# Top-k attention with a squared-ReLU MLP on one core: threshold searches dropped, GpSimd's sums re-laid, and the third replacement of 81 groups moved to SIGN and a product

## The chip, the cores and the metric

One core of a Trainium2 chip runs the whole program. The metric is device time in microseconds; lower is better. The engines are named as in the profile: PE (TensorE matmuls; PEld its weight loads), DVE (VectorE), ACT (ScalarE), POOL (GpSimd), SP (SyncE, which issues DMAs).

## The reference

Inputs are q, k, v of shape (8, 8, 576, 64) and two weights, 512 x 2048 and 2048 x 512, all float32.

```python
scores = scale * np.matmul(q, k.transpose(0, 1, 3, 2))      # 64 heads of 576 x 576
kth = np.partition(scores, -32, axis=-1)[..., -32:-31]      # each row's 32nd largest
scores = np.where(scores >= kth, scores, -1e9)
attn = softmax(scores)
x = (attn @ v), heads side by side                          # 4608 x 512
out = (np.maximum(x @ w_in, 0.0) ** 2) @ w_out              # 4608 x 512
```

## The kernel before, in words

**Groups.** The 36,864 rows of scores go in 144 groups of 256: 128 partitions hold one row of each of two heads (or, for the 64 rows left over of every head, two pairs of heads). A group's scores are 128 x 2 x 576 float32. `top_k` finds each row's 32nd largest value, the threshold `kth`; `attend` transposes the scores on PE, adds a mask (made by ACT with RELU against the threshold, L1051) and takes EXP on ACT; `fetch`, `gather` and `collect` multiply by v and normalise; `feed` runs the MLP on 256 or 128 tokens at a time, ACT taking RELU (L1242), and the square made by POOL (L1257) or ACT (L1260) as a string of letters, `SQUARES`, says.

**The order of the work.** The program is planned before it is built. Every operation is given an engine, an assumed duration, a due time and its dependencies; `Plan.schedule` walks through time, gives each engine the ready operation that is due first, and so fixes the order on every engine and every buffer. Semaphore waits are put in from the dependencies. Group n is due at `T0 + PER * n`; each kind of operation has an offset, and a further one for each of 16 stages of the run (the table `AHEAD`). PE gets filler matmuls where it would stand idle, until a time near the end.

**A threshold.** A group's tile `s` holds in each row the 576 scores and, behind them, scratch areas. The 576 scores of a row are seen as four quarters of 144.
- PE writes the scores to PSUM and ACT copies them to `s` (L820).
- DVE folds the quarters with three maximum operations (L975): `m0`, `m1`, `big`. The last is the list of 144 column maxima.
- POOL finds what the folds lost, the three lists of smaller values, without comparisons: as 32-bit integers, max + min equals the sum of the two. The first wide operation (u<-s) adds the sources of all three folds to a buffer `u`, the second (s<-u,s) subtracts the three maxima. Each is one operation over 128 x 2 x 3 x 144 elements (both L970).
- DVE takes the eight largest of the maxima (MAX8, L1014), replaces them by a very small number (L1018: a load of eight values and a MATCH_REPLACE8), and does the same two more times, over 92, 112 and 147 columns; ahead of the third time it takes the eight largest of two of the smaller lists (L1009) into the list. A last MAX8 (L1021) gives ranks 25 to 32, and so the threshold.

Tiles `s` lie in a ring of six; a group starts at column `z`, which grows smaller each time round, so that a few columns of every group are left for a check at the end.

**The searched groups.** Eight of the 144 groups (`HUNT`) get no lists. `hunt` starts from the root mean square of a row, and ACT counts, five times for each row, how many scores exceed a trial threshold: SIGN over 583 columns with its accumulator (L845); POOL corrects the trial between counts with small operations on two columns (L852). POOL then multiplies signs and scores (L884), and DVE takes eight values (L886) and picks the threshold among them. These tiles are `hs` and `hz`.

**The verdict.** At the end DVE checks all rows (ties, lists that were too short, sums that overflowed) into one flag. Where the flag is set, a plain second pass over everything follows.

Of the kernel before, what the change touches and what calls it, by code (L numbers as in the profile page):

```python
# [6 lines left out]
ALU = mybir.AluOpType  # L7
# [6 lines left out]
P = 128  # L14
# [9 lines left out]
SLAST = 760  # L24
# [4 lines left out]
SEEN = {"pe": 0.02, "act": 0.0, "dve": 0.0, "gp": 0.045, "sp": 0.08}  # L29
# [368 lines left out]
def bass_top_k_attn__then__act_relu_squared_kernel(  # L398
# [24 lines left out]
    def sb(name, shape, dt=FP32, n=None):  # L423
# [4 lines left out]
    PER = 5.247  # L428
# [8 lines left out]
    MASKS = "aaaaaaaaaaaaaaaaaaaaaaaaaaaaaaaaaaaaaaaaaaaaaaaaaaaaaaaaaaaaaaaaaaaaaaaaaaaaaaaaaaaaaaaaaaaaaaaaaaaaaaaaaaaaaaaaaaaaaaaaaaaaaaaaaaaaaaaa"  # L437
    SQUARES = "gggaggggagggagagaaggggaaggagggggaggagggagaggaaaggagggaggggggggagggaggg"
    OWN = 2
# [9 lines left out]
    WLAST = 753  # L449
# [3 lines left out]
        "av": (-25.3, -1.5, -9, -43, -22.8, -25.3, 0.1, -9.5, 17.8, -35.8, -26.9, 4.1, -14.2, -32.1, -43, -36.6),  # L453
        "copy": (-37.1, -30.2, 19, 22.4, -11.3, -34.5, 11.2, -32.3, 43.2, 43.4, 40.5, -36.4, -9, 33.4, 34.6, 45),
        "drain": (-26, 19.3, 2.6, -34.3, -16.5, 27.3, 3.4, 27.5, 3.3, 26.3, 20.3, 28.4, -43.8, -21.9, -12.4, -27.9),
        "dup": (11.7, -10, 39.6, -15.3, 40.5, 32.2, 19.9, -27.9, 37.3, -15.6, 20.8, 45, -28.9, -25.5, 29, -45),
        "end": (6.6, -7.4, 42.5, -6.2, 12.6, 35, -27.3, -13.8, -23.7, 33.7, -13.8, -11.4, -8.7, -4.4, 9.6, 18.8),
        "exp": (-12.6, -0.1, -1.1, 11.7, -11.3, -29.4, -34.4, -19.1, -11.6, -25, 7.3, 38, 19.6, 5, 22.9, 13),
        "flip": (31.6, 10.7, 14.8, -18.1, -5.6, 4.6, 41.2, -42, -40.4, -23.4, -45, 8.7, -0.5, -30.9, -43.6, -4.2),
        "fold": (-45, -32.8, -42.9, -45, -40.2, -37.7, -37.1, -24.2, -42.3, -45, -44, -31.1, -45, -42, -45, -45),  # L460
        "found": (-6.1, -10.4, -34, 23.1, 31.8, 41.7, -30.8, -23.3, -21.7, 27.5, -42.4, -34.7, -42.2, -28.9, -37.3, -42.4),
        "fourth": (-20.5, -19.8, -30.9, -10.8, -40, 20.2, -45, -10.8, -8.5, -14.6, 36.7, -28.1, -16.3, 10.7, -40.2, -7.6),
        "h": (-45, 12, -42.9, -14.4, 2.9, 23.4, 43.2, -44.5, 18, 29.8, -28.3, -14.7, 14.3, 3.5, 27.2, -23.5),
        "last": (-45, -31, -32.6, -7.3, -45, 10.3, -13.8, -45, -43, -44.6, -37.2, -39.6, 20.4, -28.9, -29.6, -44.6),
# [39 lines left out]
    HN, HA, HP, HZ, HS, HD, HO = 0.269, 0.86, 0.68, 2.18, 4.728, 29.47, 23.95  # L504
# [17 lines left out]
    c24 = sb("c24", [P, 2, NGRP + 8])  # L522
    rzall = sb("rzall", [P, NALL])
    HUNT = {(0, 2, 3): 12, (1, 2, 3): 12, (2, 2, 3): 12, (3, 2, 3): 12, (4, 2, 3): 12, (5, 2, 3): 12, (6, 2, 3): 12, (7, 0, 1): 12}
    NH = len(HUNT)
    NSTEP = 4
    GAIN, NRAW = (.016, .008, .0075, .0045), 2
    START, ROUND, ODD, FAR = 1.68, 1.5 * 2.0 ** 27, 7, 2.0 ** 53
    hk = sb("hk", [P, 12 * NSTEP + 4 + 6 + 64])
    hth = sb("hth", [P, 2, NH])  # L530
    htt = sb("htt", [P, 2, NH])
    fh = sb("fh", [P, 2, 2, NH])
    hot = sb("hot", [P, 20 + 2 * NSTEP])
    fone = sb("fone", [P, 8])
# [10 lines left out]
        "s": ([P, 2, WIDE], FP32, NF), "hs": ([P, 2 * S + 16], FP32, 2), "hz": ([P, 2 * S + 20], FP32, 1), "u": ([P, 2 * (HALF + QUART) + 4], FP32, 1), "a": ([P, 2, 8], FP32, 2),  # L545
# [5 lines left out]
    pools = {nm: Pool(nm, spec[2], turn=nm == "s") for nm, spec in sizes.items()}  # L551
# [17 lines left out]
    def at(t):  # L569
        x = mem[t.pool.name][t.slot]  # L570
        if t.pool.name in ("hs", "hz"):
            c = 8 if t.pool.name == "hs" else 10
            return x[:, c:c + 2 * S].rearrange("p (i c) -> p i c", i=2)
# [77 lines left out]
    def build(full, weights, pl):  # L651
        state = {"h": 0, "n": 0, "u": 0, "pairs": 0, "last": {}}
        kths, rzs, checks, sought = [], [], [], {}
# [129 lines left out]
        def score(gi, qks, tg, st, early=False):  # L783
# [17 lines left out]
            def scores_z():  # L801
                o = banks(ss)
                for i, j in ((0, 0), (0, 1), (1, 1), (1, 0), (2, 0), (2, 1), (3, 1), (3, 0)):
# [13 lines left out]
                  take=[ss, st], tiled=True)  # L817
# [5 lines left out]
            if early:  # L823
                return ss, [copied(0, QUART)], lambda after: copied(QUART, S, after=after)
            cp = [copied(0, S)]
            return ss, cp, None

        def hunt(k, gi, qks, tg, due):

            st, hz = tile("hs"), tile("hz")  # L830
            score(gi, qks, tg, st)
            used = [0]

            def small(n_):
                used[0] += n_
                return lambda a=0, b=n_, c=used[0] - n_: hk[:, c + a:c + b]

            def wider(t, i, n_, more):
                x = mem[t.pool.name][t.slot]
                c = 8 if t.pool.name == "hs" else 10  # L840
                return x[:, c + S * i - ODD * (more and i == 0):c + S * i + n_ + ODD * (more and i == 1)]

            def look(j, func, acc, after, bias=None, n_=S):
                kw = [dict() if bias is None else dict(bias=bias(i, i + 1), scale=-1.0) for i in range(2)]
                return [pl.op("act", HA - (S - n_) / 1200 - .09 * (j == 0), pl.at("look", due + HO + HS * j + .1 * i), lambda i=i: act.activation(  # L845
                    wider(hz, i, n_, j > 0), wider(st, i, n_, j > 0), func, accum_out=acc(i, i + 1), **kw[i]),
                    r=[st], after=after,
# [806 lines left out]
```

## Time and profile before

| | |
|---|---|
| three runs | 775.69, 775.81, 777.02 us (median 775.81) |
| the profiled run | 775.29 us, of which the span from first to last instruction is 773.4 us |
| busy: DVE, ACT, POOL, PE | 732.4, 732.5, 702.5, 706.3 us |
| granted TensorE clock | 1.00 throughout |

How the rows are read. In a table of stages a row has the stretch, its length and each engine's busy time with its count of instructions in brackets. In a table of groups a row has the line, the engine, the operation, output <- inputs, shapes and count; then the busy time in us and the mean duration in ns; then the engine's idle time just before these instructions, with what ended it. In a timeline a row has the start, the length, the engine and the operation, "x2" for two neighbours merged. A wait's row has who waited for whom, the us in total, how often, and the longest.

### The profile page before, as it was taken

Reading aid. Unit: us, or ns where it says so; the run is one execution under the profiler, and the core shown is the slowest. Engines: PE = TensorE matmul, PEld = TensorE weight load, DVE = VectorE, ACT = ScalarE, POOL = GpSimd, SP = SyncE. Lnnn points to the kernel's source line nnn. Section 1 sums busy time; section 2 is a strip of 40 time slices with the busy share of each in tenths; the row PEclk is TensorE's granted clock in tenths of the full one; section 3 lists DMA queues with packets and bytes.
Section 4 is the critical chain, followed back from the end, with each engine's and each line's share of the span. In section 5 each row is a group of like instructions: output and inputs, shape, how many; then the busy total and the mean of one; then the engine's idle time right before and its main releaser. Section 6 shows DMA issues by size and latency. Waiting matters only on the chain.

```text
span 773.4 us, 28086 instructions
## 1 busy us (share of the span) xinstructions
PE 706.3 (91%) x10764; PEld 531.8 (69%) x10764; DVE 732.4 (95%) x3504; ACT 732.5 (95%) x1173; POOL 702.5 (91%) x635
## 2 busy tenths in 40 slices
PE   7777789989998989898899999999999989999999
PEld 4555676657776676675777768677667766777676
DVE  5899999999999999999999999899999999999976
ACT  4899999999999999999999999999999999999994
POOL 3899999999989899899989999899998999999982
DMA  7677442253322451115512353123531144111111
GB/s 170 162 166 166 127 104 66 45 89 91 69 57 35 86 108 37 32 30 101 114 34 60 61 115 64 44 43 59 111 69 43 28 88 75 33 31 29 41 36 34
DMA packets 171578, 57.04 MB, mean 74 GB/s; under 512 B 156592, under 2 KB 163760, under 8 KB 171440
## 3 DMA queue, kind: packets, MB, share of 16 engines
q1 hardware_dynamic: 163376, 50.93, 28.2%
q0 software_dynamic: 7392, 4.13, 4.6%
q8 instruction: 84, 1.38, 0.8%
q14 instruction: 54, 0.44, 0.2%
q10 hardware_dynamic: 672, 0.16, 0.1%
HBM read 40.83 MB, written 13.57 MB: 70 GB/s over the span
## 4 chain that ended last, share of the span: by engine, by line
DVE 35%; POOL 30%; ACT 18%; issue 9%; PE 6%; DMA 1%; SPq 0%; POOLq 0%; DVEq 0%; ACTq 0%
POOL u L970 11%; POOL s L970 10%; DVE s L1018 10%; DVE s L975 8%; DVE c L1014 7%; PE ps L642 5%; DVE s L1009 5%; ACT s L820 4%; DVE kth L1021 4%; ACT w L1051 4%; POOL g L1257 3%; ACT p L1119 3%; ACT hz L845 2%; ACT g L1242 2%; POOL hk L852 2%
## 5 line engine op out<-in xcount | busy, mean ns | idle before, releaser
L970 POOL TENSOR_TENSOR u<-s 128x864 int32<-128x864 int32 x134 | 272.0, 2030 | 35.5 <-DVE s L975 32.0
L970 POOL TENSOR_TENSOR s<-u,s 128x864 int32<-128x864 int32 x134 | 229.5, 1713 | 5.3 <-DVE kth L1021 0.4
L1051 ACT ACTIVATE w<-s,kth 128x576 bf16<-128x576 f32 x270 | 212.1, 825 | 0.6 <-DVE kth L1021 0.4
L1018 DVE MATCH_REPLACE8 s<-c,s 128x92 f32<-128x92 f32 (+2 forms) x816 | 212.5, 268 | 0.0
L1014 DVE MAX8 c<-s 128x8 f32<-128x92 f32 (+2 forms) x816 | 194.1, 271 | 0.1
L642 PE MATMUL ps<-qk 64*128 64x384 f32 (+3 forms) x1280 | 178.3, 426 | 15.7 <-DVE s L975 14.0
L975 DVE TENSOR_TENSOR s<-ps,s 128x288 f32<-128x288 f32 x402 | 179.1, 446 | 7.7 <-ACT s L820 6.8
L1119 ACT ACTIVATE p<-ps 128x1152 bf16<-128x1152 f32 x144 | 168.8, 1173 | 1.7 <-PE ps L642 1.7
L820 ACT COPY s<-ps 128x1152 f32<-128x1152 f32 (+1 forms) x137 | 157.2, 1148 | 8.5 <-PE ps L642 7.6
L642 PEld LDWEIGHTS ps<-qk 64*128 64x128 f32 (+1 forms) x1280 | 129.6, 175 | 47.2 <-DVE s L975 23.0
L642 PE MATMUL ps<-wo,g 128*128 128x512 bf16 (+1 forms) x592 | 141.9, 375 | 2.4 <-ACT av L1187 1.0
L642 PE MATMUL ps<-xt,win 128*128 128x256 bf16 (+1 forms) x1280 | 131.8, 252 | 11.1 <-DMA xt<-x 3.9
L642 PEld LDWEIGHTS ps<-xt,win 128*128 128x128 bf16 x1280 | 97.5, 98 | 33.4 <-ACT g L1242 5.5
L1021 DVE MAX8 kth<-s 128x8 f32<-128x296 f32 x272 | 116.0, 458 | 0.0
L1009 DVE MAX8 s<-s 128x8 f32<-128x288 f32 x272 | 113.7, 451 | 0.0
L645 PEld LDWEIGHTS ps<-ident,s 64*128 64x128 f32 x2448 | 96.5, 139 | 24.6 <-ACT p L1119 8.6
L645 PE MATMUL ps<-ident,s 64*128 64x64 f32 x2448 | 103.4, 226 | 5.1 <-ACT p L1119 4.0
L1257 POOL TENSOR_TENSOR g<-g 128x1024 bf16<-128x1024 bf16 x50 | 94.8, 1896 | 4.9 <-ACT g L1242 4.9
L1242 ACT ACTIVATE g<-ps 128x512 bf16<-128x512 f32 x140 | 87.3, 654 | 3.7 <-PE ps L642 3.6
L642 PEld LDWEIGHTS ps<-wo,g 128*128 128x128 bf16 x592 | 50.9, 98 | 53.1 <-issue 4.1
L1018 DVE MATCH_VALUE_LOAD s<-c,s 128x8 f32 x816 | 65.6, 80 | 12.4 <-POOL s L970 12.1
L642 PE MATMUL ps<-vb,p 128*128 128x65 bf16 (+1 forms) x1600 | 63.0, 195 | 7.8 <-ACT g L1242 3.9
(111 smaller groups left out, 789.9 us busy)
## 6 DMA issues: line engine op xcount, KB each, us to landing
out_dram<-o SPq DMA_DIRECT2D x32, 256.0 KB, 2.3
rk<-in_k_dram SPq DMA_DIRECT2D x63, 128.0 KB, 2.6
rq<-in_q_dram SPq DMA_DIRECT2D x62, 128.0 KB, 2.6
s<-s SPq DMA_DIRECT2D x136, 32.0 KB, 1.9
g<-in_moe_w_in_dram SPq DMA_DIRECT2D x8, 512.0 KB, 4.6
g<-in_moe_w_out_dram SPq DMA_DIRECT2D x8, 512.0 KB, 4.6
vd<-in_v_dram POOLq DMA_DIRECT2D x14, 288.0 KB, 4.4
vb<-vd SPq DMA_DIRECT2D x56, 64.0 KB, 2.3
```

Of the source, the lines that this page charges most:

```text
L642: return pe.matmul(o, l, r, start=start, stop=stop, skip_group_check=True)
L645: return pe.matmul(o, i, ident, is_transpose=True, skip_group_check=True, **kw)
L820: return pl.op("act", .14 + 2 * (c1 - c0) / 1200, pl.at("copy", tg - LEAD + 1), lambda: act.copy(at(st)[:, :, c0:c1], two(banks(ss)[:, FIR ...
L970: return pl.op("gp", dur, prio, lambda: gp.tensor_tensor(o().bitcast(I32), x().bitcast(I32), y().bitcast(I32), op), **kw)
L975: return dve(.36, lambda: vec.tensor_tensor(o(), two(banks(ss)[:, FIRST_AT + c:], SECOND, QUART), x(), ALU.max), r=[ss], **kw)
L1009: prev[i] = [dve(.065 + HALF / 960, lambda i=i: vec.max(area(LIST, LIST + 8, i), area(LESS, LESS + HALF, i)), after=prev[i] + [low], hold= ...
L1014: lambda i=i, t=t, c0=c0, c1=c1: vec.max(eighth(t, i), area(c0, c1, i)),
L1018: lambda i=i, t=t, c0=c0, c1=c1: vec.match_replace(area(c0, c1, i), eighth(t, i), area(c0, c1, i), NEG), hold=[st])]
L1021: ks.append(chain(kth, i, prev[i], .065 + (8 + HALF) / 960, lambda i=i: vec.max(eighth(kth, i), area(BIGS - QUART, LIST + 8, i)), hold=[st]))
L1051: masks[i:] = [pl.op("act", .77, pl.at("mask", tw + .8 * i), lambda i=i: act.activation(at(wt)[:, i, :], at(st)[:, i, 0:S], ACTF.Relu, bia ...
L1119: return act.activation(at(pt)[:, :, :].rearrange("p c (h q) -> p h c q", h=2), bass.AP(x.tensor, x.offset, [x.ap[0], [APART, 2], [64, 9], ...
L1257: pl.op("gp", .12 + 1024 / 580, pl.at("square", tf + lag + 1), lambda g=g: gp.tensor_tensor(at(g)[:, :], at(g)[:, :], at(g)[:, :], ALU.mul ...
```

## The change

- The searches go, with their tiles, constants and small operations: all 144 groups find their threshold from lists.
- The ring of tiles `s` has seven places instead of six, in one tensor; `u` has two buffers instead of one. The scratch areas stand 194 columns apart instead of 192, and the two rows of a tile are 1250 columns apart instead of 1247.
- POOL's first wide operation now subtracts (each fold's larger source minus its result), and the second adds the other source. So the first needs all three folds; the DVE replacements wait for the first operation and no longer for the second. Groups 0 and 1, which fold on DVE alone, use the last places of the ring as scratch.
- In 81 groups (`VOIDS`: 3, 5, ..., 135 and 6, 16, ..., 136) the third replacement is not made by DVE. ACT takes SIGN of (eighth value of the third list minus value) over the 147 columns of each row, with the accumulator kept, and POOL multiplies list and signs in one operation over both rows: what is above the eighth value becomes negative, the eighth itself zero.
- The verdict reads these accumulators; equal 7th and 8th values of the third list are allowed for.
- Four of 70 squares move from POOL to ACT. `PER` goes from 5.247 to 5.15, the due time is moved on by 0.56 us for each voided group passed, filler ends 14 us earlier, and `AHEAD` holds other offsets throughout.

```diff
-SLAST = 760
+SLAST = 746
-SEEN = {"pe": 0.02, "act": 0.0, "dve": 0.0, "gp": 0.045, "sp": 0.08}
+SEEN = {"pe": 0.08, "act": 0.0, "dve": 0.0, "gp": 0.045, "sp": 0.08}
...
-    PER = 5.247
+    PER = 5.15
...
-    NF = 6
-    GAP = QUART + 48
-    ZMAX = NGRP // NF - 1
-    LESS, BIGS, LIST = S, S + 3 * QUART, S + 4 * QUART
+    NF = 7
+    GAP = QUART + 50
+    ZMAX = (NGRP - 1) // NF
+    BIGS = HALF + QUART + 3 * GAP
+    LESS, LIST = BIGS - 3 * QUART, BIGS + QUART
     WIDE = ZMAX + LIST + 8 + P // 2
...
-    HUNT = {(0, 2, 3): 12, (1, 2, 3): 12, (2, 2, 3): 12, (3, 2, 3): 12, (4, 2, 3): 12, (5, 2, 3): 12, (6, 2, 3): 12, (7, 0, 1): 12}
...
+    VOIDS = (3, 137, 2), (6, 137, 10)
...
-        "s": ([P, 2, WIDE], FP32, NF), "hs": ([P, 2 * S + 16], FP32, 2), "hz": ([P, 2 * S + 20], FP32, 1), "u": ([P, 2 * (HALF + QUART) + 4], FP32, 1), "a": ([P, 2, 8], FP32, 2),
+        "u": ([P, 2 * (HALF + QUART) + 4], FP32, 2), "a": ([P, 2, 8], FP32, 2),
...
+    PITCH = 2 * WIDE - P // 2
+    smem = sb("s", [P, NF * PITCH + P // 2])
+    mem["s"] = [smem[:, PITCH * i:PITCH * i + 2 * WIDE].rearrange("p (i c) -> p i c", i=2) for i in range(NF)]
...
-                    o_u = whole(1.685, pl.at("sums", tg - MT), ALU.add, lambda: row(u, 0, QUART, 3), lambda: row(st, HALF + QUART, GAP, 3),
-                                lambda: row(st, 0, QUART, 3), hold=[st], w=[u], take=[u], after=cp + [m0, m1])
-                    low = whole(1.685, pl.at("low", tg - ML), ALU.subtract, lambda: row(st, LESS, QUART, 3),
-                                lambda: row(u, 0, QUART, 3), lambda: row(st, HALF + QUART + GAP, GAP, 3), hold=[st, u], after=[o_u, big])
+                    o_u = whole(1.685, pl.at("sums", tg - MT), ALU.subtract, lambda: row(u, 0, QUART, 3), lambda: row(st, HALF + QUART, GAP, 3),
+                                lambda: row(st, HALF + QUART + GAP, GAP, 3), hold=[st], w=[u], take=[u], after=cp + [big])
+                    low = whole(1.675, pl.at("low", tg - ML), ALU.add, lambda: row(st, LESS, QUART, 3),
+                                lambda: row(st, 0, QUART, 3), lambda: row(u, 0, QUART, 3), hold=[st, u], after=[o_u])
...
+                    if t is c24 and not full and n in VOID:
+                        k = VOID.index(n)
+                        state["v"] += 1
+                        said = [pl.op("act", VA_, pl.at("sign", tg + VD), lambda i=i: act.activation(
+                            area(LESS + 2, LESS + 2 + c1 - c0, i), area(c0, c1, i), ACTF.Sign, bias=c24[:, i, 3 * n:3 * n + 1],
+                            scale=-1.0, accum_out=signs[:, i, k:k + 1]), hold=[st], after=prev[i]) for i in range(2)]
+                        void = pl.op("gp", VG, pl.at("void", tg + VE), lambda: gp.tensor_tensor(
+                            area(c0, c1), area(LESS + 2, LESS + 2 + c1 - c0), area(c0, c1), ALU.mult), hold=[st], after=said)
+                        checks.extend(said)
+                        prev = [[void], [void]]
+                        continue
                     for i in range(2):
-                        prev[i] = [chain(t, i, prev[i] + [low], dur + .06,
+                        prev[i] = [chain(t, i, prev[i] + [o_u], dur + .06,
                                          lambda i=i, t=t, c0=c0, c1=c1: vec.match_replace(
                                              area(c0, c1, i), eighth(t, i), area(c0, c1, i), NEG), hold=[st])]
...
-                tg = T0 + PER * (state["n"] + HN * state["h"])
+                tg = T0 + PER * state["n"] - VS * state["v"]
```

More of the change, by code (lines that the diff above doesn't have):

```diff
@@ L899, in hunted @@
-        def hunted(k, st, th, tg):
-            tw, wt = tg + PER - TW, tile("w")
-            for i in range(2):
-                pl.op("act", .77, pl.at("mask", tw + .8 * i), lambda i=i: act.activation(
-                    at(wt)[:, i, :], at(st)[:, i, 0:S], ACTF.Relu, bias=hth[:, i, k:k + 1], scale=-1.0),
-                    r=[st], w=[wt], take=[wt] if i == 0 else [], after=th)
-            return wt
         def top_k(gi, qks, tg):
@@ L913, in top_k @@
             st.phase = z = ZMAX - n // NF
-            ss, cp, copy_rest = score(gi, qks, tg, st, not (full or n))
+            ss, cp, copy_rest = score(gi, qks, tg, st, not (full or n), [state["first"][n - NF + OWN]] if not full and NF - OWN <= n < NF else [])
             dk = [0]
@@ L1029, in top_k @@
             wt, masks = tile("w"), []
-            if not full and n == NGRP - NH - 1:
+            if not full and n == NGRP - 1:
                 masks = [pl.op("act", .77, tw, lambda: act.activation(
@@ L1121, in grow @@
                     bass.AP(x.tensor, x.offset, [x.ap[0], [APART, 2], [64, 9], [1, 64]]), ACTF.Exp, scale=0.125)
-            if not full and state["n"] == NGRP - NH:
+            if not full and state["n"] == NGRP:
                 x = pl.op("pe", .6, tt - 1, turn, r=[st], w=[e], take=[e, pt], tiled=True)
@@ L1529, in verdict @@
[L1529 to L1533 removed]
+        fc = c16[:, :, 0:NGRP]
@@ new lines, in verdict, with two_, most @@
+        ends, k = [], 0
+        for j, (v0, v1, step) in enumerate(VOIDS):
+            n_ = len(range(v0, v1, step))
+            said = signs[:, :, k:k + n_]
+            sixth, seventh, eighth = (c24[:, :, 3 * v0 + d:3 * (v0 + step * (n_ - 1)) + d + 1:3 * step] for d in (2, 1, 0))
+            k += n_
+            def two_(o, x, y, op, **kw):
+                return pl.op("dve", .25, 1e6, lambda: vec.tensor_tensor(o, x, y, op), **kw)
+            def most(c, x, op, **kw):
+                return pl.op("dve", .25, 1e6, lambda: vec.tensor_reduce(fone[:, c:c + 1], x, AX.XY, op), **kw)
+            x = two_(seventh, seventh, eighth, ALU.is_equal, after=checks)
+            y = two_(said, said, seventh, ALU.subtract, after=[x])
+            z = two_(sixth, sixth, eighth, ALU.is_le, after=checks)
+            x, y, z = most(5 + 3 * j, said, ALU.max, after=[y]), most(6 + 3 * j, said, ALU.min, after=[y]), most(7 + 3 * j, sixth, ALU.max, after=[z])
+            ends += [z, pl.op("dve", .1, 1e6, lambda j=j: vec.tensor_scalar(fone[:, 5 + 3 * j:7 + 3 * j], fone[:, 5 + 3 * j:7 + 3 * j], AWAY, None, ALU.not_equal), after=[x, y])]
@@ new lines, in verdict @@
+        done = [pl.op("dve", .4, 1e6, lambda: vec.tensor_tensor(fc, kth[:, :, 0:NGRP], fc, ALU.is_gt), after=[x])]
+        done += [pl.op("dve", .2, 1e6, lambda s=s: vec.tensor_tensor(
+            c8[:, :, s:NGRP:NF], mem["s"][s][:, :, ZMAX + LIST + 7:ZMAX + LIST + 7 - len(range(s, NGRP, NF)):-1], kth[:, :, s:NGRP:NF], ALU.is_gt), after=[x], order=squared) for s in range(NF)]
+        done = [pl.op("dve", .4, 1e6, lambda: vec.tensor_tensor(fc, fc, c8[:, :, 0:NGRP], ALU.max), after=done)]
+        ends.append(pl.op("dve", .35, 1e6, lambda: vec.tensor_reduce(fone[:, 0:1], fc, AX.XY, ALU.max), after=done))
```

264 lines of the change are left out of this document (81 added, 183 removed).

## The prediction

> **What bounds the kernel now.** I read the head of the page first, then the table of stages, the waits, and the groups of instructions with their shapes kept apart.
>
> ```profile
> span 773.4 us, 28086 instructions
> PE 706.3 (91%) x10764; PEld 531.8 (69%) x10764; DVE 732.4 (95%) x3504; ACT 732.5 (95%) x1173; POOL 702.5 (91%) x635
> ...
> DVE 35%; POOL 30%; ACT 18%; issue 9%; PE 6%; DMA 1%; SPq 0%; POOLq 0%; DVEq 0%; ACTq 0%
> ```
>
> No single engine bounds it. DVE and ACT are busy for 95% of the span, POOL for 91%, and the chain that ended last (third line) changes between these three all the way. So I make a floor for each engine: its own work, plus the idle time at the two ends that nothing in the change touches. The stages separate the ends from the middle:
>
> ```profile
> 0.00:60.00 60.00, 46.21 (x546) 30.62 (x546) 49.30 (x227) 46.94 (x74) 43.41 (x90) 1.00 0.67 163
> 60.00:740.00 680.00, 628.65 (x9732) 477.54 (x9732) 660.17 (x3176) 663.36 (x1061) 643.95 (x535) 1.00 0.32 68
> 740.00:773.40 33.40, 31.45 (x487) 23.61 (x487) 22.90 (x103) 22.18 (x40) 15.19 (x12) 1.00 0.12 40
> ...
> 520.00:620.00 100.00, 96.77 (x1438) 71.61 (x1436) 97.42 (x473) 99.56 (x159) 94.01 (x76) 1.00 0.30 60
> ```
>
> After the length the columns are PE, PEld, DVE, ACT, POOL, then the granted clock (1.00 everywhere). At the ends DVE idles (60 − 49.30) + (33.4 − 22.90) = 21.2 us, ACT 13.1 + 11.2 = 24.3 us, POOL 16.6 + 18.2 = 34.8 us. In the middle they idle 19.8, 16.6 and 36.1 us. So today's floors are DVE 732.4 + 21.2 = 753.6, ACT 756.8 and POOL 737.3, and the span stands 17 us above the highest, since three nearly full engines make each other wait. The last row shows how full ACT can be: 99.56% over 100 us. The waits behind the idle time (us in total, times, longest):
>
> ```profile
> POOL u L970 <- DVE s L975: 32.0, 27, 9.5
> DVE s L1018 <- POOL s L970: 12.1, 15, 3.0
> DVE hk L886 <- POOL hz L884: 4.2, 6, 1.2
> ACT hz L845 <- POOL hk L852: 5.5, 8, 1.5
> ACT hz L845 <- POOL htt L852: 1.6, 4, 0.7
> ```
>
> The first two are the two halves of one exchange: POOL waits for DVE's folds, and DVE's first replacement (L1018) waits for POOL's second sum. The last three belong to the threshold searches alone.
>
> **The change, engine by engine.** Groups whose shapes carry the prices:
>
> ```profile
> L970 POOL TENSOR_TENSOR u<-s 128x864 int32<-128x864 int32 x134 | 272.0, 2030 | 35.5 <-DVE s L975 32.0 <-DVE hz L1531 1.0
> L970 POOL TENSOR_TENSOR s<-u,s 128x864 int32<-128x864 int32 x134 | 229.5, 1713 | 5.3 <-DVE kth L1021 0.4
> L884 POOL TENSOR_TENSOR hz<-hz,hs 128x576 f32<-128x576 f32 x16 | 19.2, 1200 | 0.8 <-ACT hz L845 0.8
> L886 DVE MAX8 hk<-hz 128x8 f32<-128x576 f32 x16 | 12.1, 757 | 4.3 <-POOL hz L884 4.2
> L1260 ACT ACTIVATE g<-g 128x1024 bf16<-128x1024 bf16 x20 | 22.6, 1128 | 0.0
> L1257 POOL TENSOR_TENSOR g<-g 128x1024 bf16<-128x1024 bf16 x50 | 94.8, 1896 | 4.9 <-ACT g L1242 4.9
> L1031 ACT ACTIVATE w<-s,kth 128x576 bf16<-128x576 f32 x1 | 0.8, 775 | 0.5 <-DVE kth L1021 0.5
> L1034 ACT ACTIVATE w<-s,kth 128x64 bf16<-128x64 f32 x1 | 0.3, 348 | 0.0
> L1523 DVE TENSOR_TENSOR c<-s,kth 128x46 f32<-128x46 f32 x4 | 0.8, 237 | 0.0
> L700 ACT ACT_TABLE_LOAD x1 | 1.3, 1283 | 2.0 <-issue 2.0
> ```
>
> Neighbours on an engine overlap by about 0.1 us, so durations over-count; where I can I take the distance from one start to the next in a dense stretch.
>
> *DVE.* The rows of the timeline (start, length):
>
> ```profile
> 300.06 0.45 DVE L975 TENSOR_TENSOR s<-ps,s 128x288 f32<-128x288 f32 x1
> 300.41 0.09 DVE L1018 MATCH_VALUE_LOAD s<-c,s 128x8 f32 x1
> ...
> 300.69 0.09 DVE L1018 MATCH_VALUE_LOAD s<-c,s 128x8 f32 x1
> ...
> 301.72 0.41 DVE L1014 MAX8 c<-s 128x8 f32<-128x92 f32 x2
> ...
> 306.86 0.41 DVE L1014 MAX8 c<-s 128x8 f32<-128x92 f32 x2
> ```
>
> Between 301.72 and 306.86, without idle, DVE issues exactly one group's work: 5.14 us. A third replacement with its load takes 300.69 − 300.41 = 0.28 us. The eight groups that were searched become ordinary ones: +8 × 5.14 = +41.1 us. In 81 groups (67 from 3 by 2, and 14 from 6 by 10) both rows lose the third replacement: −162 × 0.28 = −45.4 us. The searches' wide MAX8 go: −12.1 us (L886). Net −16.4 us, so 716.0 us. The verdict gets 16 small instructions and loses 4; by L1523 (0.237 us) that is about 2.9 us, placed in the end stage, where DVE idles 10.5 of 33.4 us; I take nothing for it, and 2.9 us if they stand ahead of the flag on the path. DVE's floor: 716.0 + 21.2 = 737.2 us.
>
> *ACT.*
>
> ```profile
> 306.45 0.45 ACT L845 ACTIVATE hz<-hs 128x288 f32<-128x288 f32 x1
> ...
> 306.89 0.43 ACT L845 ACTIVATE hz<-hs 128x288 f32<-128x288 f32 x1
> ...
> 311.27 0.78 ACT L845 ACTIVATE hz<-hs,hk 128x583 f32<-128x583 f32 x1 [0.17 <-POOL hk L852]
> 311.96 0.19 ACT L845 ACTIVATION_READ_ACCUMULATOR hz<-hs,hk 128x1 f32 x1
> 312.05 1.11 ACT L1119 ACTIVATE p<-ps 128x1152 bf16<-128x1152 f32 x1
> ...
> 328.87 1.09 ACT L1260 ACTIVATE g<-g 128x1024 bf16<-128x1024 bf16 x1
> 329.82 0.63 ACT L1242 ACTIVATE g<-ps 128x512 bf16<-128x512 f32 x1
> ```
>
> A search's SIGN over 583 columns with its accumulator read holds ACT from 311.27 to 312.05, 0.78 us; a SQUARE over 288 takes 0.44 us. A search has five SIGN looks and one SQUARE for each of two rows, so eight have 80 of the first and 16 of the second: −62.4 − 7.0 = −69.4 us. The new SIGN is the same form over 147 columns. A column costs (775 − 348)/512 = 0.834 ns (L1031, L1034), so it takes 0.78 − 436 × 0.000834 = 0.416 us; from the SQUARE, which has no bias operand, it would be 0.44 − 141 × 0.000834 = 0.322 us. I take 0.416, the same form: +162 × 0.416 = +67.4 us (low end 52.2). The one table load in the whole trace, with SIGN, EXP and RELU mixed, says that SIGN brings none. The string of squares has 46 "g" in 70 instead of 50, so four squares go to ACT: +4 × (329.82 − 328.87) = +3.8 us. Net +1.8 us: 734.3 us, floor 758.6 us. ACT gains nothing from the change, and has the highest floor after it.
>
> *POOL.* The busy time of the searches' small steps, L852, alone:
>
> ```profile
> 0.00:773.40 773.40, 35.82 (x160) 1.00 0.34 74
> ```
>
> and from the timeline a square with its successor:
>
> ```profile
> 302.95 1.90 POOL L1257 TENSOR_TENSOR g<-g 128x1024 bf16<-128x1024 bf16 x1
> 304.80 1.72 POOL L970 TENSOR_TENSOR s<-u,s 128x864 int32<-128x864 int32 x1
> ```
>
> Small steps and the searches' products (L884) go: −35.8 − 19.2 = −55.0 us. Four squares leave: −4 × 1.85 = −7.4 us. The product that voids the third list has 294 elements. Between the rows of 576 and 864 elements whose sources stand two columns apart, an element costs (1713 − 1200)/288 = 1.78 ns, so it takes 1200 − 282 × 1.78 = 698 ns: +81 × 0.70 = +56.7 us.
>
> Now the wide sums. Today the first (u<-s) reads columns 432, 624, 816 of a group's tile beside 0, 144, 288: the difference is a multiple of four, and it takes 2030 ns. The second reads u at a phase of z + 2 modulo 4 beside the tile at z: two apart in the first row of the tile, an odd distance in the second row (1247 columns on, against 432 in u). It takes 1713 ns. After, the first sum reads 432 + 194k beside 626 + 194k, two apart in both rows: I take 1713. The second reads u beside the tile's start; in the first row two apart, but the tile's second row is now 1250 columns on, so there both sources fall on the same column modulo 4. If that alone makes the price, half of it is slow: (1713 + 2030)/2 = 1.87 us; if it is only how a source starts, 1.71. I take 1.71, as in the same instruction today, and keep 1.87. Sums: 142 × 3.426 = 486.5 us against 501.5, −15.0 us (or +7.5). POOL in all: 702.5 − 55.0 − 7.4 + 56.7 − 15.0 = 681.8 us, floor 716.6 us (739 with the slow half). Both are under ACT's.
>
> The Trainium skill has a rule that speaks against this part: its page GPSIMD Engine Reference, section 3.1 (Elementwise, side-by-side cycle accounting), puts a two-input operation at about 2.6 cycles an element because both inputs share one read port, wherever they lie; from its 4497 ns at 2048 elements, an estimate for 864 is 1.90 us for either sum, and moving sources would gain nothing. The trace has 2030 and 1713 ns for equal shapes, above and below that. What the rule would do to the time is the second rival.
>
> *Waits that move.* The first sum now waits for all three folds, not two (0.36 us more, by the fold that starts at 300.06 and its successor at 300.41). POOL stands 42 us under ACT's floor, so that is free until its waits, 32.0 us today, grow by more than this. DVE's first replacement now waits for the first sum, not the second, which takes away most of the 12.1 us; next late is the MAX8 over the lower values (L1009), four instructions later. A seventh tile lets scores run one group further ahead, and the second u lets POOL start a sum before the last is done with. PE, its loads and SP's issues keep their work; PE loses filler only.
>
> **The sum.** ACT's floor is 758.6 us. Of its 16.6 us idle in the middle, 7.1 were waits for the searches' small steps, so 9.5 us is the most that stays of them. With DVE 16 us and POOL 21 us lighter I expect what the fullest 100 us show, 0.44% of about 668 us, 2.9 us: a span of 761.5 us. The profiled run took 775.29 us, 1.9 us over its span (0.5 below the median of the three runs, 775.81): 763.4 us.
>
> **Rivals.** (1) *ACT keeps its idle time.* With 9.5 us in the middle the span is 768.1 us, the time 770.0. For it: ACT waits on PE and DVE too, not on the searches alone. Against: 520 to 620 us.
>
> (2) *The column isn't the price.* If the sums cost 2030 and 1713 by add and subtract, or by u being the output, POOL has 142 × 0.317 = 45.0 us more: 726.8 us, floor 761.6, above ACT's. With 8 us of its waits left (it had 36.1) that is a span of 769.6 and a time of 771.5. By the skill's 1.90 us for both sums, an estimate, the floor would be 769.7 us. Against it: L884, a float product of two tiles two columns apart, goes with the 1713 ns sum on a line that leaves 174 ns at no elements, near a small step (35.82/160 = 0.22 us); with the 2030 ns sum it would leave less than nothing.
>
> (3) *Slower: the new loop through three engines is exposed.* In a voided group DVE's last MAX8 comes after two SIGNs on ACT and a product on POOL: 2 × 0.416 + 0.70 = 1.5 us and three hand-overs, and ACT's queue stands behind a SIGN that waits for DVE. Fully exposed that is 81 × 1.5 = 122 us. From ACT's floor there are 773.4 − 758.6 = 14.8 us to lose, 0.18 us a voided group; from there it is slower. At a quarter exposed (30 us) the time is 791 us. For it: DVE already waits 12.1 us for POOL. Against: these are 15 waits in 134 groups, with a loop as long; DVE has 5 us of other groups to do meanwhile.
>
> (4) *The flag.* If a row failed the verdict, the plain second pass would run: 144 groups of eight 576-wide MAX8 (0.757) are 870 us on DVE alone. Worked out from the reference's inputs, no row has more than 7 values above its threshold among the 288 lower ones, where 8 fit.
>
> **Chances.** The forecast 0.70, rival 1 0.10, rival 2 0.08, rival 3 0.07, the second pass 0.02, and 0.03 for DVE bounding, with cheap SIGNs: ACT at 0.322 has a floor of 743.4 us, DVE's 737.2 us plus 3.5 us of remaining waits and the verdict's 2.9 gives 743.6, a time of 746. The range takes the forecast from half the cheap SIGN (−7.6 us) to rivals 1 and 2: 756 to 772 us. No change means within 0.2%, 1.6 us, about what a measurement of this kernel can tell. Rivals 1 and 2 end in part there (0.04); slower are rival 3 mostly and the second pass (0.08).
>
> **What would show it.** u<-s near 1.71 us, s<-u,s at 1.71 or 1.87; the SIGN with its read 0.4 us from start to start; DVE busy near 716 to 719 us, ACT 734, POOL 680 to 705; ACT over 99% from 60 us on; DVE's wait for POOL's sums under 5 us. The prediction is wrong if ACT idles more than 10 us in the middle, if DVE's kth waits for the product for more than 5 us in all, or if the first sum stays at 2 us.

## The result and the profile after

The changed kernel takes 763.92 us (median of four runs, 762.64 to 764.21) against 776.0 us before (four runs, 775.69 to 777.02): a ratio of 0.984 [0.982, 0.986], 12 us less. The forecast was 763.4 us. The profiled run took 762.64 us, 1.8 us over its span, at a granted clock of 1.00. One run of e10 below and one of the kernel before beside it were far slower, at granted clocks of 0.65 and 0.75, and are left out of all figures.

The head of the page and the shares of the chain of waits:

```profile
span 760.8 us, 27790 instructions
PE 694.7 (91%) x10681; PEld 529.1 (70%) x10750; DVE 723.4 (95%) x3369; ACT 730.7 (96%) x1309; POOL 705.3 (93%) x530
...
POOL 38%; ACT 24%; DVE 19%; PE 9%; issue 7%; DMA 1%; SPq 1%; POOLq 0%; DVEq 0%; ACTq 0%
```

Against the kernel before, DVE lost 9.0 us of work, ACT 1.8, and POOL gained 2.8, where I had POOL losing 21. The largest share of the chain has moved from DVE to POOL, not to ACT. The stages, with the columns as in the prediction (length, PE, PEld, DVE, ACT, POOL):

```profile
0.00:60.00 60.00, 48.60 (x593) 33.26 (x595) 50.97 (x231) 45.89 (x77) 42.82 (x64) 1.00 0.67 163
60.00:740.00 680.00, 630.67 (x9851) 483.35 (x9918) 658.01 (x3086) 675.32 (x1216) 658.28 (x464) 1.00 0.33 69
740.00:760.80 20.80, 15.47 (x243) 12.51 (x242) 14.45 (x56) 9.46 (x19) 4.20 (x4) 0.96 0.10 33
...
520.00:620.00 100.00, 94.48 (x1409) 69.61 (x1421) 95.54 (x448) 100.00 (x183) 96.99 (x70) 1.00 0.36 67
```

ACT is busy for 675.32 of the middle's 680 us, and for all of the stretch that was 99.56% full before. By itself this says that ACT is the bound; the experiments contradict that. The groups of instructions that the change touches:

```profile
L891 POOL TENSOR_TENSOR s<-s,u 128x864 int32<-128x864 int32 x142 | 265.2, 1871 | 4.2
L891 POOL TENSOR_TENSOR u<-s 128x864 int32<-128x864 int32 x142 | 244.7, 1723 | 25.9 <-DVE s L896 24.8
L1188 POOL TENSOR_TENSOR g<-g 128x1024 bf16<-128x1024 bf16 x46 | 87.0, 1893 | 2.3 <-ACT g L1173 1.9
L939 ACT ACTIVATE s<-s,c 128x147 f32<-128x147 f32 x162 | 72.5, 477 | 0.3 <-DVE c L934 0.3
L942 POOL TENSOR_TENSOR s<-s 128x294 f32<-128x294 f32 x81 | 57.2, 706 | 2.6 <-ACT s L939 2.5
L968 DVE TENSOR_SCALAR w<-s,kth 128x512 bf16<-128x512 f32 x1 | 2.1, 2136 | 0.0
```

The first sum went from 2030 to 1723 ns, the second from 1713 to 1871, and the product takes 706 ns against 698 worked out. SIGN's 477 ns is a duration that overlaps its neighbours; the timeline gives its cost from start to start:

```profile
404.32 0.44 ACT L939 ACTIVATE s<-s,c 128x147 f32<-128x147 f32 x1
404.63 0.22 ACT L939 ACTIVATION_READ_ACCUMULATOR s<-s,c 128x1 f32 x1
404.73 0.43 ACT L939 ACTIVATE s<-s,c 128x147 f32<-128x147 f32 x1
405.04 0.21 ACT L939 ACTIVATION_READ_ACCUMULATOR s<-s,c 128x1 f32 x1
405.13 1.45 ACT L982 ACTIVATE w<-s,kth 128x576 bf16<-128x576 f32 x2
```

404.32 to 404.73 to 405.13: 0.41 and 0.40 us for a SIGN with its read. The waits (us in total, times, longest):

```profile
POOL u L891 <- DVE s L896: 24.8, 23, 11.4
ACT s L818 <- PE ps L640: 10.0, 9, 2.0
DVE s L949 <- POOL u L891: 7.0, 9, 1.6
DVE s L929 <- POOL s L891: 4.9, 10, 1.1
DVE kth L952 <- POOL s L942: 4.7, 11, 1.1
```

DVE's wait for POOL's sums has split in two, 7.0 us ahead of the first replacement and 4.9 ahead of the MAX8 over the lower values: 11.9 us, as much as the 12.1 before.

### The profile page after: what moved, and what is told of

It reads as the page before. It is cut to its first block, busy times and chain, and to the rows that moved or that the text cites. A ratio compares the mean times of both kernels' runs of the same rounds, so it can differ in the third digit from the quotient of the medians.

```text
span 760.8 us, 27790 instructions
## 1 busy us (share of the span) xinstructions
PE 694.7 (91%) x10681; PEld 529.1 (70%) x10750; DVE 723.4 (95%) x3369; ACT 730.7 (96%) x1309; POOL 705.3 (93%) x530
## 4 chain that ended last, share of the span: by engine, by line
POOL 38%; ACT 24%; DVE 19%; PE 9%; issue 7%; DMA 1%; SPq 1%; POOLq 0%; DVEq 0%; ACTq 0%
POOL u L891 14%; POOL s L891 13%; PE ps L640 7%; ACT w L982 6%; ACT p L1050 5%; ACT s L818 5%; DVE s L896 5%; POOL g L1188 4%; DVE s L949 4%; DVE kth L952 3%; POOL s L942 3%; DVE c L934 3%; ACT g L1173 3%; DVE s L929 3%; ACT s L939 2%
## 5 line engine op out<-in xcount | busy, mean ns | idle before, releaser
L891 POOL TENSOR_TENSOR s<-s,u 128x864 int32<-128x864 int32 x142 | 265.2, 1871 | 4.2
L891 POOL TENSOR_TENSOR u<-s 128x864 int32<-128x864 int32 x142 | 244.7, 1723 | 25.9 <-DVE s L896 24.8
L982 ACT ACTIVATE w<-s,kth 128x576 bf16<-128x576 f32 x286 | 226.8, 837 | 0.6 <-DVE kth L952 0.6
L896 DVE TENSOR_TENSOR s<-ps,s 128x288 f32<-128x288 f32 x432 | 191.6, 443 | 4.4 <-ACT s L818 3.4
L640 PE MATMUL ps<-qk 64*128 64x192 f32 (+3 forms) x1280 | 178.2, 425 | 12.4 <-DVE s L896 10.7
L818 ACT COPY s<-ps 128x1152 f32<-128x1152 f32 (+1 forms) x145 | 169.0, 1166 | 10.9 <-PE ps L640 10.0
L949 DVE MATCH_REPLACE8 s<-c,s 128x112 f32<-128x112 f32 (+2 forms) x702 | 176.8, 258 | 0.1
L640 PE MATMUL ps<-wo,g 128*128 128x512 bf16 (+1 forms) x523 | 126.8, 373 | 11.0 <-issue 4.6
L929 DVE MAX8 s<-s 128x8 f32<-128x288 f32 x288 | 119.1, 448 | 5.3 <-POOL s L891 4.9
L939 ACT ACTIVATE s<-s,c 128x147 f32<-128x147 f32 x162 | 72.5, 477 | 0.3 <-DVE c L934 0.3
L640 PEld LDWEIGHTS ps<-vb,p 128*128 128x128 bf16 (+1 forms) x1600 | 53.6, 100 | 21.8 <-ACT av L1118 4.6
(91 smaller groups left out, 760.3 us busy)
```

What stands on the lines that cost most here:

```text
L640: return pe.matmul(o, l, r, start=start, stop=stop, skip_group_check=True)
L818: return pl.op("act", .14 + 2 * (c1 - c0) / 1200, pl.at("copy", tg - LEAD + 1), lambda: act.copy(at(st)[:, :, c0:c1], two(banks(ss)[:, FIR ...
L891: return pl.op("gp", dur, prio, lambda: gp.tensor_tensor(o().bitcast(I32), x().bitcast(I32), y().bitcast(I32), op), **kw)
L896: return dve(.36, lambda: vec.tensor_tensor(o(), two(banks(ss)[:, FIRST_AT + c:], SECOND, QUART), x(), ALU.max), r=[ss], **kw)
L929: prev[i] = [dve(.0685 + HALF / 960, lambda i=i: vec.max(area(LIST, LIST + 8, i), area(LESS, LESS + HALF, i)), after=prev[i] + [low], hold ...
L949: lambda i=i, t=t, c0=c0, c1=c1: vec.match_replace(area(c0, c1, i), eighth(t, i), area(c0, c1, i), NEG), hold=[st])]
```

## The experiments

Three theories were in play. A, the prediction's: ACT alone sets the end. B: the exchange between POOL and DVE does. A2, formed when both had fallen: ACT and POOL, and after them DVE, are bounds of about the same height, so that reliefs of several engines gain more than their sum; its rival C says that something else holds the time, and that each relief is worth its 2 to 3 us and they only add up. All times below are medians; e1 to e4, e5 to e8 and e9 to e12 each shared one chip, and each ratio is to runs of the kernel before on that chip. Differences in us from the changed kernel are from its 763.92 us, measured apart from these; e12, the same kernel, took 0.9 us less.

| kernel | us | ratio to before [95%] |
|---|---|---|
| e1 columns right in row two as well | 761.35 | 0.980 [0.977, 0.983] |
| e2 sums back on one column | 794.70 | 1.024 [1.021, 1.027] |
| e3 ACT 11 us lighter | 762.01 | 0.981 [0.978, 0.984] |
| e4 DVE 11 us lighter | 762.10 | 0.982 [0.979, 0.984] |
| e5 e1 and e3 | 758.17 | 0.976 [0.974, 0.978] |
| e6 e1, e3 and e4 | 755.67 | 0.972 [0.970, 0.974] |
| e7 14 voided groups, not 81 | 789.48 | 1.018 [1.016, 1.020] |
| e8 kernel before, POOL 41 us lighter | 765.66 | 0.986 [0.985, 0.988] |
| e9 e1, and the last square behind the last mask | 759.30 | 0.979 [0.977, 0.981] |
| e10 e9, and eight squares from ACT to POOL | 768.93 | 0.991 [0.989, 0.993] |
| e11 changed, last square behind the last mask | 762.01 | 0.982 [0.981, 0.984] |
| e12 changed kernel again | 763.01 | 0.983 [0.981, 0.985] |

**Columns.** In e1 a tile's rows are 1252 columns apart instead of 1250, so that both rows of both sums have their sources two apart; nothing else moves.

```diff
-    WIDE = ZMAX + LIST + 8 + P // 2
+    WIDE = ZMAX + LIST + 8 + P // 2 + 2
```

> A tile's two rows stand 1252 columns apart instead of 1250, so that the second wide sum reads its sources two columns apart in both rows; the order of work on every engine is the one of the changed kernel. Placement theory: the second sum falls from 1.87 to 1.72 us, 142 times, so POOL's work falls by 21 us; if how a source starts is what counts, it stays at 1.87. For the time: theory A (ACT is the bound in the middle of the run, 760.8 us span) says 757 to 761 us of span, since POOL was not what ACT waited for; theory B (the exchange between POOL and DVE is the bound, as POOL's 38% of the last chain has it) says 10 to 20 us less, 741 to 751.

Its groups, and its page:

```profile
L891 POOL TENSOR_TENSOR u<-s 128x864 int32<-128x864 int32 x142 | 244.5, 1722 | 36.9 <-DVE s L896 36.3
L891 POOL TENSOR_TENSOR s<-s,u 128x864 int32<-128x864 int32 x142 | 242.7, 1712 | 4.2
```

```profile
PE 697.3 (92%) x10681; PEld 531.2 (70%) x10750; DVE 724.6 (95%) x3369; ACT 729.8 (96%) x1309; POOL 683.4 (90%) x530
...
ACT 74%; DVE 9%; PE 8%; issue 5%; POOL 3%; DMA 1%; SPq 1%; ACTq 0%
```

The second sum falls from 1871 to 1712 ns and the first stays: one row of the two had been slow. POOL is 22 us lighter, its waits for DVE's folds take up 11.5 of that (24.8 to 36.3), and the time falls by 2.6 us, with an interval that still touches the changed kernel's. Now ACT has 74% of the chain, which is what I had forecast for the change itself.

e2 puts 192 columns instead of 194 between the first sum's sources, a multiple of four in both rows; the tile's rows come to 1246 columns, 814 more than u's 432, so that the second sum is two apart in the first row and on the same column in the second.

```diff
-    GAP = QUART + 50
+    GAP = QUART + 48
...
+    WIDE = ZMAX + LIST + 8 + P // 2 + 2
```

> The scratch areas stand 192 columns apart again and the tile's rows 1246, so that the first wide sum (still a subtraction) reads both sources on the same column modulo four, and the second keeps its half; the order of work is that of the changed kernel. Placement theory: first sum back to 2.03 us, second at 1.87. If it were subtract against add, the first stays at 1.72. Theory A: POOL has 142 x 0.31 = 44 us more, 749 us with some 34 us of idle at the ends, so POOL becomes the bound and the span is 783 to 795 us, slower than before the change. If POOL's load is hidden: 761 to 765.

```profile
L891 POOL TENSOR_TENSOR u<-s 128x864 int32<-128x864 int32 x142 | 288.8, 2034 | 19.5 <-DVE s L896 17.7
L891 POOL TENSOR_TENSOR s<-s,u 128x864 int32<-128x864 int32 x142 | 264.9, 1869 | 4.2
```

```profile
PE 704.8 (89%) x10681; PEld 533.8 (67%) x10750; DVE 726.3 (92%) x3369; ACT 738.9 (93%) x1309; POOL 747.6 (94%) x530
...
POOL 64%; DVE 17%; issue 8%; ACT 7%; PE 4%; SPq 0%; DMA 0%; POOLq 0%; DVEq 0%
```

The first sum is still a subtraction into u, and takes 2034 ns: the column is the price, and not the operation. Without the columns, the rest of the change is slower than the kernel before by 18 us (in an order of instructions that was written for the fast sums), and 31 us slower than the change as made. POOL is then the bound: 747.6 us of work, 64% of the chain.

**Is it ACT, or POOL with DVE?** e3 halves the columns of ACT's 24 squares and leaves the other half unsquared, e4 takes 36 columns off the MAX8 over the lower values and leaves those values out; each keeps every instruction in its place.

```diff
 e3
-                        at(g)[:, :], at(g)[:, :], ACTF.Square), u=[g])
+                        at(g)[:, 0:512], at(g)[:, 0:512], ACTF.Square), u=[g])
 e4
-                                area(LIST, LIST + 8, i), area(LESS, LESS + HALF, i)),
+                                area(LIST, LIST + 8, i), area(LESS, LESS + HALF - 36, i)),
```

> The 24 squares that ACT makes take only half of their columns (the other half of those hidden values stays unsquared): 24 x 0.43 = 10.2 us less work on ACT, order unchanged. Theory A (ACT bounds): span 8 to 10 us shorter, 751 to 753. Theory B (POOL and DVE bound): under 3 us, 758 to 761.

> The MAX8 over the lower values reads 252 instead of 288 columns in each of 288 instructions (the last 36 of two lower lists are left out): 288 x 0.0375 = 10.8 us less work on DVE, order unchanged. Theory A (ACT bounds): under 3 us, span 758 to 761. Theory B (the exchange of POOL and DVE): 5 to 11 us shorter, 750 to 756.

The groups show the edits taking hold, L1191 of e3 and L929 of e4 (448 ns before the edit):

```profile
L1191 ACT ACTIVATE g<-g 128x512 bf16<-128x512 bf16 x24 | 15.8, 660 | 0.0
```

```profile
L929 DVE MAX8 s<-s 128x8 f32<-128x252 f32 x288 | 108.2, 410 | 6.0 <-POOL s L891 5.5
```

Both gain about 1.9 us, e3 for 24 × (1.10 − 0.66) = 10.6 us of work, and with intervals that overlap the changed kernel's. The stages of e3 show where ACT's relief went:

```profile
60.00:740.00 680.00, 631.77 (x9862) 484.12 (x9927) 657.68 (x3089) 669.84 (x1216) 658.45 (x464) 1.00 0.33 69
```

ACT's idle time in the middle has grown from 4.7 to 10.2 us: it waits more instead of ending sooner. A has fallen, which had asked e3 for 8 to 10 us, and B with it, which had asked e1 for 10 us or more and e4 for 5 or more.

ACT's busy time fell by 5.9 us only (730.7 to 724.8), although 10.6 us of work had gone. Busy time also covers short waits. In the changed kernel:

```profile
531.00 2.14 ACT L982 ACTIVATE w<-s,kth 128x576 bf16<-128x576 f32 x3
533.00 0.62 ACT L1209 COPY o<-ps 128x512 f32<-128x512 f32 x1
```

These three masks start 0.67 us apart, and a mask lasts 0.84 us in the mean, so one that starts 0.17 us late leaves no idle time. An estimate from the starts in the traces, with each kind of instruction priced at the lower quartile of its distances to the next start: of the middle's 680 us ACT's work leaves about 16 in the changed kernel and 26 in e3. By this ACT was some 98% full, not over 99%.

**Several at once.** e5 has the edits of e1 and e3, e6 those of e1, e3 and e4, as shown above.

> Both reliefs at once: the tile rows 1252 columns apart (POOL 22 us lighter) and the 24 ACT squares on half of their columns (ACT 10.2 us lighter; the other half stays unsquared); order unchanged. Each alone took 2 to 3 us off. Theory A2 (ACT and POOL are two bounds of about the same height, so that relieving one uncovers the other): the two together take more than their sum, 8 to 12 us, a time of 752 to 756 us. Rival C (something else, DVE or PE's order, holds the time and each relief only trims waits): 758 to 760, the sum of the two.

> As the run beside it, and the MAX8 over the lower lists on 252 instead of 288 columns (DVE 10.8 us lighter, 36 values of each pair of lower lists left out). A2 says that after ACT and POOL, DVE is the next bound: 4 to 9 us under the run without it. If PE or the transfers come next: under 2 us.

e5 gains 5.7 us on the changed kernel and e6 8.2, for the single gains 2.6, 1.9 and 1.8: sums of 4.5 and 6.3. That is C's reading for the most part, little more than the sum, and the spread of a kernel's runs, up to 4 us, doesn't tell the excess from none. A2 had expected more, 752 to 756 us for e5 against 758.2 measured, and 4 to 9 us from e5 to e6, which differ by 2.5. e7 and e8 below came out in A2's ranges (786 to 795 and 763 to 768 us), so neither theory fits all four runs, and what bounds the changed kernel stays open. What takes up the rest, when all three are 10 to 22 us lighter, I have not found.

**Load instead of relief.** e7 takes 67 groups out of the voided ones, which gives DVE 134 replacements back and takes 134 SIGNs and 67 products away. Its order is worked out anew by the same rules, with later due times: each voided group had set the due times behind it 0.56 us earlier.

```diff
-    VOIDS = (3, 137, 2), (6, 137, 10)
+    VOIDS = (6, 137, 10),
```

> Only the 14 groups 6, 16, ..., 136 are voided by SIGN and product; the other 67 get their third replacement on DVE again, and the order is planned anew with the same offsets. DVE has 134 x 0.28 = 37.5 us more, ACT 134 x 0.41 = 55 us less, POOL 67 x 0.70 = 47 us less. Theory A2: DVE becomes the only bound: 723.4 + 37.5 = 761 us busy with 15 us of idle at the ends, and 8 to 15 us of waits: a time of 786 to 795 us, slower than before the change. Rival (the three-engine loop of the voided groups costs what it saves): 760 to 770.

```profile
PE 713.5 (91%) x10907; PEld 544.3 (69%) x10966; DVE 756.2 (96%) x3630; ACT 689.4 (88%) x1041; POOL 664.0 (84%) x463
```

25.6 us slower than the changed kernel, for DVE's 134 × 0.28 = 37.5 us, while ACT and POOL are each 41 us lighter. So load on one engine is paid for at about two thirds to three quarters (e2: 31 us for POOL's 42), although e7's new order has a part in it, and relief at an eighth to a fifth (e1, e3, e4). With these offsets, once the searches are gone the voids are needed: with 14 of them DVE is the fullest engine and the change is slower than before.

**Where the gain comes from.** e8 is the kernel before, with POOL's 50 squares over half their columns and the other half left unsquared.

```diff
-                        at(g)[:, :], at(g)[:, :], at(g)[:, :], ALU.mult), u=[g])
+                        at(g)[:, 0:512], at(g)[:, 0:512], at(g)[:, 0:512], ALU.mult), u=[g])
```

> The kernel before, in its own order, with POOL's 50 squares on half of their columns (the other half stays unsquared): 50 x 0.86 = 43 us less work on POOL, as much as the wide sums lose in the change by their columns. What POOL's relief alone was worth to the old kernel: if POOL was a bound there beside DVE and ACT (A2), 8 to 13 us, a time of 763 to 768 us, because DVE's 12.1 us of waits for POOL go; if DVE and ACT bounded it alone, under 3 us, 773 or more.

```profile
PE 695.9 (91%) x10694; PEld 532.0 (70%) x10764; DVE 731.8 (96%) x3504; ACT 730.8 (96%) x1173; POOL 661.2 (87%) x635
```

```profile
DVE s L1018 <- POOL s L970: 5.7, 5, 3.0
```

10.5 us for POOL's 41, with DVE and ACT as before: a relief of POOL alone brings the old kernel to within 2 us of the changed one, and halves DVE's wait for it (12.1 us before).

This shows what POOL's relief was worth in the old kernel, not where the change's 12 us come from: there POOL's work did not fall (702.5 to 705.3 us), because the products and the sums of eight more groups took what the columns and the searches gave. What the traces show is DVE 9.0 us lighter and ACT's idle time in the middle down from 16.6 to 4.7 us, of which 7.1 were waits for the searches' small steps. The seventh tile, the second `u`, the earlier start of the replacements and the new offsets were not tried apart.

**A version that beats both.** The timeline of the changed kernel's end has an oddity: the last mask on DVE (L968) takes 2.14 us, and a square on POOL runs beside it. The group of the same form before took 0.49 us:

```profile
L1037 DVE TENSOR_SCALAR w<-s,kth 128x512 bf16<-128x512 f32 x1 | 0.5, 486 | 0.0
```

The end of the changed kernel:

```profile
742.21 1.97 POOL L1188 TENSOR_TENSOR g<-g 128x1024 bf16<-128x1024 bf16 x1 [1.04 <-ACT g L1173]
742.33 2.14 DVE L968 TENSOR_SCALAR w<-s,kth 128x512 bf16<-128x512 f32 x1
...
743.86 0.37 ACT L965 ACTIVATE w<-s,kth 128x64 bf16<-128x64 f32 x1
...
745.08 0.28 PE L640 MATMUL ps<-steep_bf,w 64*128 64x64 bf16 x8
...
745.82 0.13 DVE L1442 TENSOR_SCALAR fone<-fone 128x2 f32<-128x2 f32 x1
...
747.08 0.23 PE L643 MATMUL ps<-ident_bf,x 128*128 128x128 bf16 x1 [0.99 <-POOL x L1127]
```

e9 is e1 with that square made to wait for the mask; e11 has this edit alone, without e1's columns; e12 is the changed kernel on the same chip; e10 adds to e9 that eight of ACT's 24 squares are made by POOL, at the same places in the order.

```diff
 e9, e10, e11, after the order is planned
+    (ts,) = [o for o in main.order["dve"] if o.dur == .501]        # DVE's last mask
+    sq = [o for o in main.order["gp"] if o.start < ts.start][-1]   # POOL's last square before it
...
+    sq.deps.add(ts)
+    sq.start, sq.end = ts.end + .01, ts.end + .01 + sq.end - sq.start
 e10, ahead of that
...
+    MOVE = 8
+    for o, fn in sorted(act_squares, key=lambda x: -room(x[0]))[:MOVE]:
+        main.order["act"].remove(o)
+        o.eng, o.fn = "gp", fn
+        main.order["gp"].append(o)
+        main.order["gp"].sort(key=lambda p: p.start)
```

> Tile rows 1252 columns apart, and POOL's square that ran beside the last group's mask on DVE now waits for that mask. In the changed kernel this mask (TENSOR_SCALAR over 512 columns) took 2.14 us and ended 0.3 us after POOL's square; in the kernel before it took 0.49 us, beside no such operation. If the two shut each other out, the mask falls to 0.49 us and the end of the run comes 1.6 us sooner, as it is on the way to the last scores: a time of 759 to 760.5 us with the spread rows (which alone gave 761.4). If the length of the mask is its own: 2.1 us, and 761 to 762.

> As the run beside it, and eight of the 24 squares of ACT are made by POOL at the same place in the order: ACT 8 x 0.95 = 7.6 us lighter, POOL 8 x 1.85 = 14.8 us heavier, so POOL is still 7 us under the changed kernel. By the runs so far a relief of ACT by 10 us with spread rows took 3.2 us off and POOL's 22 us took 2.6 us off: 0 to 2.5 us under the run beside it. If POOL's operations are now in the way of the wide sums: 1 to 4 us over it.

> The changed kernel with only the square at the end waiting for the last mask: mask 0.49 us instead of 2.14 and 1.6 us off the time, 762.0 to 762.8 beside 763.9; no change if the mask's length is its own.

> The changed kernel itself, for comparison on one chip: 763 to 764.5 us.

The end of e11, in the timeline:

```profile
742.41 0.48 DVE L968 TENSOR_SCALAR w<-s,kth 128x512 bf16<-128x512 f32 x1
...
742.97 2.31 POOL L1188 TENSOR_TENSOR g<-g 128x1024 bf16<-128x1024 bf16 x1 [1.73 <-DVE w L968]
...
743.93 0.37 ACT L965 ACTIVATE w<-s,kth 128x64 bf16<-128x64 f32 x1
...
744.23 1.07 DVE L1442 TENSOR_SCALAR fone<-fone 128x2 f32<-128x2 f32 x1
...
745.15 0.28 PE L640 MATMUL ps<-steep_bf,w 64*128 64x64 bf16 x8
...
746.57 0.23 PE L643 MATMUL ps<-ident_bf,x 128*128 128x128 bf16 x1 [0.41 <-POOL x L1127]
```

The mask is 1.66 us shorter, but PE multiplies by the masks at 745.15 instead of 745.08: it was not waiting for them. What PE waits for is POOL's product `x` (L1127), 0.99 us at 747.08 and 0.41 at 746.57; that stands behind DVE's division (L1125), and this behind the mask and small instructions of the verdict. On this way the stall has moved: the square, now later, runs beside one of those, L1442, which takes 1.07 us instead of 0.13. So of the 1.66 us some 0.5 are left. e11's 762.01 us cannot be told from e12's 763.01. e9 is the version that beats both: 759.30 us; its mean lies 3.2 ± 2.0 us below e12's on the same chip, and e1's 2.6 us make up most of that.

e10 missed: 9.6 us slower than e9, where 1 to 4 were the most expected. Its page and two waits that were 5.9 and 2.0 us in e9:

```profile
PE 696.5 (91%) x10681; PEld 530.4 (69%) x10750; DVE 722.1 (94%) x3369; ACT 724.7 (95%) x1301; POOL 698.4 (91%) x538
```

```profile
DVE s L949 <- POOL u L891: 10.2, 11, 1.6
DVE s L929 <- POOL s L891: 5.8, 6, 1.4
```

POOL carries 698.4 us, less than in the changed kernel (705.3), and yet the time is 5 us above it. So the amount of POOL's work doesn't explain it; that DVE waits 8.1 us longer for the two sums points to where the squares stand. The trace bears it out: at four of the eight moved squares DVE then waits 1.4 to 1.9 us, 6.3 in all, for the sum or product right behind the square in POOL's queue, where e9's DVE doesn't wait (for one, a square from 246.43 us, the first sum behind it from 248.28, and DVE's replacement held for 1.56 us until 250.03). It was not tried by putting them elsewhere.

## Why the prediction was right, and where it was not

*The number.* Its floors were nearly exact. ACT: 730.7 us of work, 25.4 us idle at the ends (60 − 45.89 and 20.8 − 9.46) and 4.7 in the middle make the span of 760.8; the forecast had 734.3, 24.3 and 2.9. Its errors, 3.6 us too much and 1.1 and 1.8 too little, nearly cancel, so that the number came out to 0.5 us by some luck. It holds as a sum, not as a cause.

*"ACT has the highest floor after it", so ACT sets the end: the step that failed.* The floor was the highest, by 17 us over DVE's and POOL's, but 10.6 us off ACT gave 1.9 us. The floor was made of busy time, which covers short waits as shown at e3, so ACT had some 16 us to spare in the middle where the profile has 4.7 idle. ACT's queue takes its work in a fixed order from PE and DVE, and in e3 its gaps opened elsewhere as its work shrank. Among the variants of the changed kernel ACT came to lead the chain clearly only where POOL was lighter (74% in e1, 67% in e9). What sets the end in place of ACT alone is open: no relief of one engine in the changed kernel gave more than 2.6 us.

*POOL's sums.* The first was right (1723 against 1713). For the second I took 1.71 and kept 1.87; 1.871 was measured, and 142 × (1.871 − 1.713) = 22.4 us takes the forecast 681.8 to 704.2, where 705.3 is the busy time. The reason given for the alternative, the second row on the same column, is shown by e1. The 22 us cost little, 2.6 us by e1. The Trainium skill (GPSIMD Engine Reference, section 3.1) puts a two-input operation at about 2.6 cycles an element. Taken as holding wherever the sources lie, as the prediction took it, that is an estimate of 1.90 us for either sum, and the columns could have brought nothing; 1712 against 2034 ns for the same shapes contradict that.

*DVE.* 723.4 us against 716.0. The mask beside the square is 1.65 us of the difference, the verdict's larger number of small instructions about 2.5 by their groups; the other 3 I have not traced.

*ACT.* SIGN at 0.40 to 0.41 us from start to start, 0.416 forecast; there is no second table load.

*Waits.* "DVE's wait for POOL's sums under 5 us" was wrong: 11.9 us. As forecast the MAX8 over the lower values became the next late one (4.9), but the first replacement still waits 7.0 us, perhaps because the sum that it waits for now waits for the third fold; that was not tried apart. The product holds kth up for 4.7 us in 11 waits of 81 groups (5.8 us in e12, the same kernel, just over the 5 us named as a sign of being wrong): the loop through three engines is hardly exposed, and rival 3, which needed 15 us and more, is out. Rival 1's 9.5 us of idle time did not come in the profile's count, 4.7 us. Rival 2 falls with e1 and e2, where the same subtraction takes 1722 or 2034 ns by its columns alone. Of rival 4, a second pass, there is no trace: 27790 instructions, fewer than before.

*The verdict and the end.* I took nothing for them. The last kth starts 17.2 us from the end of the span before (756.20 of 773.4) and 19.5 after (741.29 of 760.8): 2.3 us longer, near the 2.9 us that were kept as the alternative. But this is not the verdict's instructions alone: the mask beside the square, 1.65 us longer than before, stands on the way to the end. Without it the end is 18.9 us (e11, 741.36 of 760.3), 1.7 more than before, and that still holds the stall of L1442.

## What to carry to other kernels

When three engines are 91 to 96% full, the highest floor can give the time and still not be what bounds it; take 10 us off that engine alone, in place, before calling it the bound, and count work from start to start, as busy time covers short waits. Price load and relief apart: here load on one engine cost two thirds of itself or more, and relief gave an eighth to a quarter. When operands are placed by column for an engine's sake, work the placement out for every row of the tile, not the first one; and moving work to an engine with slack can cost (9.6 us in e10), here because it stands ahead of sums that DVE waits for, as far as the trace tells.

## What the hardware showed that I had not expected

A POOL sum of two sources costs 2034 ns for 864 elements when they fall on the same column of four bytes modulo four, 1712 when two apart, and 1869 to 1871 when one of the two rows is on the same column: half the extra price for half the elements.

A DVE instruction can stand still for the length of a POOL instruction: the mask took 2.14 us beside a square that had started 0.12 us earlier, and 0.48 without; L1442, on two columns, took 1.07 us beside the square in e11, and 0.13 without. The Trainium skill says so (SBUF — State Buffer, section Who interferes with whom): DVE in some modes shares a pair of ports with GpSimd, and the one that comes later waits for the whole instruction. The traces agree.
